# Fused forgetting attention and SwiGLU kernel: all spare TensorE matmuls left out, the order unchanged

## The chip, the cores and the metric

The kernel runs on one core of a Trainium2 chip. The metric is the device time of one execution in microseconds. The profile is of one such execution; its span is counted from the first to the last instruction.

## The reference

For each of 8 batches and 8 heads, with 576 positions of 64 values, attention with a decay that comes from a forget gate f:

```python
scores = scale * np.matmul(q, k.transpose(0, 1, 3, 2))
log_f = np.log(np.clip(f, 0.0001, 1.0))
cum = np.cumsum(log_f, axis=-1)
decay = cum[:, :, :, None] - cum[:, :, None, :]
scores = np.where(causal, -1000000000.0, scores + decay)
attn = softmax(scores)            # with 1e-09 in the denominator
attn_out = np.matmul(attn, v)
```

The heads are put side by side to x of 4608 tokens by 512, and a feed-forward layer of width 1536 follows:

```python
xn = x / np.sqrt(np.mean(x * x, axis=-1, keepdims=True) + 1e-06) * rms_g
g = xn @ w_gate
out = (g / (1.0 + np.exp(-g)) * (xn @ w_val)) @ w_out
```

Inputs and output are float32; the matmuls of the kernel run in bf16 with float32 sums.

## The kernel before, in words

The whole program is a list of 1,551 small pieces of work. Each piece (a load, a cast, a set of transposes, a block of scores, an exponential, and so on) is made by `plan.add` with its engine, an estimate of its duration, and the buffers it takes and frees. The order in which the pieces are issued is not computed when the kernel is built: it is written out in the string `ORDER` (lines 22 to 102), and `Plan.run` (line 153) goes through its words one after the other. Each engine and each DMA queue therefore works in the order of the words that belong to it; waits between engines follow from the data and the buffers.

A word has a name and may have suffixes. `@A`, `@D`, `@O` and `@S` choose the engine (ScalarE, VectorE, GpSimd, SP), `:ff` chooses a PSUM pool, and `*N` asks for spare matmuls ahead of the piece. The names that matter here, with batch first:

- `Lq`, `Lk`, `Lv`, `Lqk`: loads of q, k, v and of the last 64 positions into float32 stage tiles `st` (10 buffers), most on SP's queue, some on ScalarE's. `Lv1.3` is the load of the fourth v tile of batch 1. `Cq`, `Ck`, `Cqk`: casts of these tiles to bf16 (`ld`).
- `tr`, `trt`: transposes of q and k on TensorE (batches 0 to 2 only; lines 530, 521 and 552) into a `ff` tile; `keeptr` copies them into `QK` (line 222 by way of the helper `copy`).
- `far`: opens the PSUM tile of a block of scores of batch 0 with the causal bias, 4 matmuls (line 664). `sc`: scores of head pairs (line 679; two heads lie in the two halves of the partitions). `esc`: exponentials on ScalarE (line 688). `msc`: the causal mask on GpSimd (line 694), for batch 1 on. `sc0.0.384` holds the last block of all four head pairs in one tile, and four exponentials read it.
- `turn_dec`, `keep_dec`: the decay factors, turned on TensorE and copied to `decT` by VectorE (lines 301, 304). `Sv`: v times these factors into `Vs` (lines 451, 452), on VectorE for batch 0 and mostly on GpSimd later.
- `val`: values (line 714), `xpo`: their division into `X` by VectorE (lines 721, 722), `sq`, `rs`, `xn`: the RMS norm (lines 729, 735, 739), `xtr`: its transpose on TensorE for batches 0 and 1 (line 766), which `kxtr` copies to `xT`.
- `g`, `v…f`, `th`, `ga`, `hga`: gate and value matmuls (line 863), tanh on ScalarE, and the two products on VectorE (lines 872, 879), for groups of 512 tokens (the first two groups are halves). `pj`, `o`, `so`: the output projection (line 889), its copy and its store.
- `turn_rg`, `spread_rg`: the norm's weights turned and spread on TensorE (lines 357, 366). `wg`, `wv`, `wo`: loads of the weights by GpSimd's queue.

The first 60 us or so hold the start of the attention, where loads, casts, transposes and scores of batch 0 depend on one another. Later the feed-forward matmuls of the batches done so far fill TensorE between pieces of attention.

A piece that opens a PSUM tile calls `warm_up` (lines 249 to 253) on it. If its word has `*N`, this issues N // 4 matmuls of 512 columns and N % 4 of 128 columns on a tile `idle` of zeros. They write to the tile that the piece overwrites directly after, so they have no effect on the output. Fill for a score tile is issued where the tile is opened (`open_sc`, line 654), fill for `v0.2f` at the head of `gate` (line 858).

```python
k = st.pop("fill", 0)
for w in [4] * (k // 4) + [1] * (k % 4):
    x = bass.AP(tensor=idle.tensor, offset=idle.offset, ap=[idle.ap[0], [0, w], [1, 128]])
    nc.tensor.matmul(ps[:, 0:w * 128], lhsT=idle, rhs=x, start=True, stop=True)
```

Of the kernel before, what the change touches and what calls it, by code (L numbers as in the profile page):

```python
# [14 lines left out]
B, H, S, D = 8, 8, 576, 64  # L15
# [4 lines left out]
NP = H // 2  # L20

ORDER = """
one Lq0.0@A far Lk0.0 Lqk01 lf ident Lq0.1@A Lqk00 rg identb clear Lq0.2@A Lk0.1 far0.1.0*16 fetch_ln Ck0.0@A Lk0.2 Cq0.0 Lv0.0 tr0.01*20 clip tr0.00
log turn_rg Lv0.1 keep_rgT keeptr0.01.q keeptr0.00.k spread_rg keeptr0.01.k@D keeptr0.00.q@A Lk0.3@A scan far0.0.0 Lq0.3@A Cqk0 Cq0.1 fetch trt0*4
Lv0.40 sc0.0.0 sc0.1.0 Ck0.1 keeptrt0 Lv0.3 Cq0.2@D esc0.0.0 keep_rg@D expo Ck0.2@O far0.3.0 tr0.03 tri esc0.1.0 tr0.10 twice Lv0.41 keeptr0.03.k
turn_dec k4.0@D Lk1.0@A tr0.02 keep_dec sc4.0 Ck0.3@O keeptr0.03.q@A Lk1.1 Cq0.3@A Sv0.0 Lqk10 keeptr0.02.k@A tr0.12*8 keeptr0.10.k@D exp4.0 Lq1.0
Lv0.2@A sc0.3.0 Sv0.1@O keeptr0.12.k@D Lqk11 esc0.3.0 keeptr0.10.q sc0.0.384*4 wg0 esc0.3.384 keeptr0.02.q far0.1.1024 esc0.0.384 sc0.1.1024
esc0.1.384 wv0 esc0.2.384 val0.2.0 Lq1.1 val0.6.0:ff esc0.1.1024 far0.2.0 Lq1.3 xpo0.6.0 wg1 sc0.2.0 Lk1.3 keeptr0.12.q esc0.2.0 sc0.1.512 Sv0.4@O
val0.0.0:ff xpo0.2.0 esc0.1.512 far0.3.1024 xpo0.0.0 val0.4.0 sc0.3.1024 Sv0.3 Ck1.1@A mask4.0 far0.2.1024 Lk1.2 esc0.3.1024 sc0.2.1024 xpo0.4.0
Lv1.41 Sv0.2 sq0.1 Lq1.2 sq0.0 val0.3.2*8 Lv1.40 Cq1.0@D esc0.2.1024 val0.2.2:ff rs0.0 sc0.0.512 Ck1.0 esc0.0.512 xn0.0 far0.0.1024 sc0.0.1024 Lv1.1  # L30
Cqk1 esc0.0.1024 sc0.2.512 xn0.1 wv1 trt1*2 tr1.0 esc0.2.512 xpo0.2.2 Cq1.1 keeptrt1 xtr0.1 keeptr1.0.q@A wg2 xpo0.3.2 xtr0.0 Lq2.0 keeptr1.0.k
sc0.3.512 kxtr0.1@D val0.4.2 kxtr0.0 esc0.3.512 val0.5.2:ff k4.1@D val0.1.2:ff Cq1.3@A tr1.1 xpo0.1.2 Lv1.0 sc1.0.512 keeptr1.1.k xpo0.5.2 val0.0.2:ff
esc1.0.512 xpo0.4.2 val0.7.2:ff xpo0.0.2 val0.6.2 keeptr1.1.q@A xpo0.7.2 sc4.1 g0.0 esc1.0.0 xpo0.6.2 Ck1.3 v0.0f th0.0 sq0.3 g0.2 ga0.0 sq0.4 Ck1.2
tr1.3 exp4.1 wv2 sq0.2 keeptr1.3.q sc1.0.1024*2 th0.2 hga0.0 rs0.2 esc1.1.512 ga0.2 v0.2f*3 xn0.3 Lv1.2 keeptr1.3.k g0.4 hga0.2 Cq1.2@A xn0.2 xtr0.3
th0.4 v0.4f kxtr0.3@D esc1.0.1024 ga0.4 tr1.2 xtr0.2 keeptr1.2.q@A sc1.1.0 kxtr0.2 esc1.1.0 keeptr1.2.k@D g1.0 Sv1.4 hga0.4 esc1.1.1024 v1.0f Lv1.3
xn0.4 msc1.0.1024 th1.0 g0.6 Lk2.0@A Lqk21 ga1.0 sc1.2.512 th0.6 Lqk20 hga1.0 g1.2 esc1.2.0 ga0.6 v1.2f th1.2 esc1.2.512 ga1.2 g1.4 hga1.2 xtr0.4
Lq3.3 Sv1.1 th1.4 sc1.2.1024 kxtr0.4 Lk2.1@A ga1.4 v0.6f wo0 esc1.3.512 v1.4f hga0.6 Lq2.1 mask4.1 esc1.2.1024 g1.6 Cq2.0 hga1.4 Sv1.0 g0.8 th1.6
# [928 lines left out]
```

## Time and profile before

| what | value |
|---|---|
| median of 5 runs | 381.08 us (380.41 to 383.15) |
| the profiled execution's own time | 381.05 us |
| its span | 379.2 us |
| mean granted TensorE clock | 0.99 |
| DMA | 52.58 MB, mean 139 GB/s |
| spare matmuls (line 253) | 22, from 1.1 to 38.5 us |

The page gives busy time by engine, a row of 40 slices of the span (9.5 us each) with busy tenths and the granted clock of TensorE in tenths, and the chain of work that ended last, followed back from the last instruction. The trace can be asked for the instructions of one engine in a stretch, with the idle time ahead of each in square brackets and the instruction that ended it. Ends of matmuls are modelled: a row's length includes the way through the array, so rows of successive groups overlap. Starts are what to compare.

### The profile page before, as it was taken

How to read it: one execution, taken by the hardware profiler on the slowest of the kernel's cores; microseconds unless marked ns; L12 is line 12 of the kernel's file. 1: busy time of each engine (PE TensorE's matmuls, PEld its weight loads, DVE VectorE, ACT ScalarE, POOL GpSimd, SP SyncE). 2: the span in 40 equal slices, each digit the busy share in tenths (PEclk: the TensorE clock that was granted, in tenths of full speed). 3: DMA queues.
4: the chain of work that ended last, by engine and by line, in shares of the span. 5: the costliest groups of instructions: out<-in, count | busy, mean ns of one | idle time of the engine just before them, and what ended most of it. 6: DMA issues, size and time to landing. Idle time of an engine off the chain costs nothing.

```text
span 379.2 us, 8155 instructions
## 1 busy us (share of the span) xinstructions
PE 366.8 (97%) x3136; PEld 195.5 (52%) x3136; DVE 260.2 (69%) x500; ACT 220.2 (58%) x368; POOL 136.2 (36%) x247
## 2 busy tenths in 40 slices
PE   7889999999999999999999999999999999999996
PEld 3557778454644544455454544454445544444443
DVE  4777977849858778568856865688367876863560
ACT  4599876688696487444845585447466423323312
POOL 3763825337467144625342474021720111000001
PEclk9699999999999999999999999999999999999999
DMA  8999999996699899998959893741300234002003
GB/s 203 249 242 234 206 223 187 216 200 150 143 203 168 187 186 181 206 144 173 182 129 207 157 193 83 170 63 42 85 28 16 57 85 122 3 0 83 29 0 112
DMA packets 144774, 52.58 MB, mean 139 GB/s; under 512 B 128188, under 2 KB 141120, under 8 KB 144736
## 3 DMA queue, kind: packets, MB, share of 16 engines
q1 hardware_dynamic: 128512, 36.98, 50.3%
q0 software_dynamic: 6016, 8.79, 11.1%
q10 hardware_dynamic: 10208, 6.31, 6.8%
q8 instruction: 24, 0.39, 0.4%
q14 instruction: 14, 0.11, 0.1%
HBM read 37.90 MB, written 9.44 MB: 125 GB/s over the span
## 4 chain that ended last, share of the span: by engine, by line
PE 80%; DMA 10%; POOL 3%; DVE 2%; ACT 2%; issue 1%; SPq 0%; POOLq 0%; ACTq 0%; DVEq 0%
PE ff L863 45%; PE ff L889 22%; DMA st<-in_v_dram 5%; PE po L714 5%; PE sc L679 5%; PE ff L714 2%; DMA st<-in_k_dram 2%; DMA st<-in_q_dram 2%; DMA out_dram<-ores 1%; POOL PT L694 1%; POOL Vs L451 1%; ACT PT L688 1%; DVE xn L739 1%; PE ff L766 1%; POOL rs L735 1%
## 5 line engine op out<-in xcount | busy, mean ns | idle before, releaser
L868 ACT ACTIVATE th<-ff 128x512 f32<-128x512 f32 x108 | 64.5, 597 | 94.5 <-PE ff L863 92.0
L863 PE MATMUL ff<-xT,wv 128*128 128x512 bf16 (+1 forms) x480 | 110.9, 358 | 0.6 <-DVE ga L872 0.6
L863 PE MATMUL ff<-xT,wg 128*128 128x512 bf16 (+1 forms) x480 | 110.8, 358 | 0.4 <-ACT QK L222 0.2
L688 ACT ACTIVATE PT<-sc 128x1024 bf16<-128x1024 f32 (+2 forms) x100 | 95.7, 990 | 14.1 <-PE sc L679 13.5
L872 DVE SCALAR_TENSOR_TENSOR ga<-th,ff 128x512 f32<-128x512 f32 x108 | 73.9, 685 | 39.9 <-ACT th L868 39.1
L889 PE MATMUL ff<-wo,hT 128*128 128x512 bf16 (+1 forms) x444 | 98.2, 373 | 0.0
L879 DVE SCALAR_TENSOR_TENSOR hT<-ga,ff 128x512 bf16<-128x512 f32 x108 | 73.7, 684 | 14.8 <-PE ff L863 8.2
L863 PEld LDWEIGHTS <-wg 128*128 128x128 bf16 x480 | 45.1, 98 | 44.0 <-issue 1.9
L889 PEld LDWEIGHTS <-hT 128*128 128x128 bf16 x444 | 42.4, 98 | 47.9 <-issue 1.4
L863 PEld LDWEIGHTS <-wv 128*128 128x128 bf16 x480 | 44.5, 98 | 43.5 <-issue 3.4
L694 POOL TENSOR_SCALAR_AFFINE_SELECT PT<-PT 128x256 bf16<-128x256 bf16 (+1 forms) x84 | 42.4, 529 | 65.9 <-ACT PT L688 65.5
L714 PEld LDWEIGHTS <-PT 128*128 128x128 bf16 x896 | 33.7, 98 | 12.4 <-issue 2.1
L739 DVE SCALAR_TENSOR_TENSOR xn<-X,rs,rgb 128x512 bf16<-128x512 f32 x40 | 32.6, 842 | 7.9 <-POOL rs L735 7.8
L897 POOL DMA_DIRECT2D out_dram<-ores x16 | 9.2, 577 | 70.5 <-ACT ores L222 38.4
L222 ACT COPY ores<-ff 128x512 f32<-128x512 f32 (+1 forms) x25 | 14.2, 569 | 34.1 <-PE ff L889 30.0
L222 POOL CAST ld<-st 128x512 bf16<-128x512 f32 x32 | 21.1, 670 | 24.9 <-DMA st<-in_q_dram 14.3
L451 POOL TENSOR_TENSOR Vs<-st,decT 128x512 bf16<-128x512 f32 x21 | 23.3, 1109 | 15.1 <-DMA st<-in_v_dram 13.1
L679 PE MATMUL sc<-QK 64*128 64x256 bf16 (+3 forms) x272 | 28.5, 294 | 0.2 <-ACT PT L688 0.2
L735 POOL TENSOR_TENSOR rs<-sq,mhalf 128x5 f32<-128x5 f32 (+2 forms) x9 | 10.1, 1119 | 51.6 <-ACT junk L729 48.1
L729 ACT ACTIVATE junk<-X 128x513 bf16<-128x513 f32 x40 | 25.4, 634 | 1.7 <-DVE X L722 1.2
L714 PE MATMUL po<-Vs,PT 128*128 128x65 bf16 x577 | 24.8, 193 | 1.0 <-POOL PT L694 0.9
L679 PEld LDWEIGHTS <-QK 64*128 64x128 bf16 x528 | 13.5, 95 | 17.0 <-issue 11.9
(89 smaller groups left out, 259.1 us busy)
## 6 DMA issues: line engine op xcount, KB each, us to landing
st<-in_v_dram SPq DMA_DIRECT2D x28, 256.0 KB, 4.5
st<-in_q_dram SPq DMA_DIRECT2D x27, 256.0 KB, 4.4
st<-in_k_dram SPq DMA_DIRECT2D x26, 256.0 KB, 4.4
out_dram<-ores POOLq DMA_DIRECT2D x15, 256.0 KB, 3.4
out_dram<-ores SPq DMA_DIRECT2D x12, 256.0 KB, 2.3
out_dram<-ores ACTq DMA_DIRECT2D x8, 256.0 KB, 2.6
st<-in_k_dram ACTq DMA_DIRECT2D x6, 256.0 KB, 5.5
wo<-in_moe_w_out_dram POOLq DMA_DIRECT2D x2, 768.0 KB, 9.5
```

Source lines behind the costliest of these rows:

```text
L222: {"DVE": nc.vector.tensor_copy, "POOL": nc.gpsimd.tensor_copy, "ACT": nc.scalar.copy}[eng](o, x)
L451: e.tensor_tensor(Vs[i][:, j, :, 0:D], t, bcast(dj, D), ALU.mult)
L679: nc.tensor.matmul(sc[:, par, c:c + n], lhsT=k_cols(r, p, kj), rhs=q_cols(r, p, q0, n), start=not opened, stop=not opened or (kj, q0) == b ...
L688: nc.scalar.activation(T["pt", b, p][:, :, c0:c0 + n], T.pop(("sc", b, p, c0))[:, :, 0:n], ACT.Exp, scale=scale)
L694: nc.gpsimd.affine_select(out=d, in_=d, pattern=[[0, n], [1, 128]], compare_op=ALU.is_ge, fill=0.0, base=0, channel_multiplier=-1)
L714: nc.tensor.matmul(T["po", b, hs][:, qm, m, :], lhsT=w, rhs=Vs[i][:, kj, h, :], start=(kj == 0), stop=(kj == qi))
L739: nc.vector.scalar_tensor_tensor(xn, in0=X[i][:, j, 0:DM], scalar=T["rs", b, js][:, j:j + 1], in1=rgb, op0=ALU.mult, op1=ALU.mult)
L863: nc.tensor.matmul(ps[:, c * w:c * w + w], lhsT=wt[:, dc, (fc + c) * 128:(fc + c + 1) * 128], rhs=T["xT", g][:, dc, 0:w], start=(dc == 0), ...
L868: nc.scalar.activation(t, T["pg", g, fc], ACT.Tanh, scale=0.5)
L872: nc.vector.scalar_tensor_tensor(a, in0=T.pop(("th", g, fc)), scalar=1.0, in1=T.pop(("pg", g, fc)), op0=ALU.add, op1=ALU.mult)
L879: nc.vector.scalar_tensor_tensor(o, in0=T.pop(("ga", g, fc)).rearrange("p (c t) -> p c t", t=w), scalar=0.5, in1=T.pop(("pv", g, fc)).rear ...
L889: nc.tensor.matmul(po, lhsT=T["hT", g][:, fc, j * 128:(j + 1) * 128], rhs=wo[:, fc, c0:c1], start=(fc == 0), stop=(fc == NFC - 1))
```

## The change

All `*N` suffixes go; no word is moved, added or taken away. Nine words had one: `far0.1.0*16`, `tr0.01*20`, `trt0*4`, `tr0.12*8`, `sc0.0.384*4`, `val0.3.2*8`, `trt1*2`, `sc1.0.1024*2` and `v0.2f*3`, together 15 matmuls of 512 columns and 7 of 128. `warm_up` and the memset of `idle` stay. Cut to the words that differ:

```diff
-... far0.1.0*16 fetch_ln ... tr0.01*20 clip tr0.00
+... far0.1.0 fetch_ln ... tr0.01 clip tr0.00
-... fetch trt0*4
+... fetch trt0
-... tr0.12*8 keeptr0.10.k@D exp4.0 Lq1.0
+... tr0.12 keeptr0.10.k@D exp4.0 Lq1.0
-... sc0.0.384*4 wg0 ...
+... sc0.0.384 wg0 ...
-... val0.3.2*8 Lv1.40 ...
+... val0.3.2 Lv1.40 ...
-... trt1*2 tr1.0 ...
+... trt1 tr1.0 ...
-... sc1.0.1024*2 th0.2 ... v0.2f*3 xn0.3 ...
+... sc1.0.1024 th0.2 ... v0.2f xn0.3 ...
```

## The prediction

> **What bounds the kernel now.** I read the page first, then the chain of waits in order of time, then the stretch to 60 us engine by engine.
>
> ```profile
> PE 366.8 (97%) x3136; PEld 195.5 (52%) x3136; DVE 260.2 (69%) x500; ACT 220.2 (58%) x368; POOL 136.2 (36%) x247
> ...
> PEclk9699999999999999999999999999999999999999
> ...
> PE 80%; DMA 10%; POOL 3%; DVE 2%; ACT 2%; issue 1%; SPq 0%; POOLq 0%; ACTq 0%; DVEq 0%
> ```
>
> TensorE is busy 97% of 379.2 us, and the chain that ended last is 80% TensorE. But the spare matmuls all lie between 1.1 and 38.5 us, and there it is other things. The chain, from the view of the chain of waits (start, us, what):
>
> ```profile
> 15.13 0.50 DVE decT L304
> ...
> 16.35 0.94 DVE Vs L452
> 17.29 1.18 DVE QK L222 x2
> ...
> 36.03 19.19 DMA st<-in_v_dram
> ...
> 55.29 1.04 POOL Vs L451
> ...
> 56.49 1.29 POOL PT L694 x3
> ```
>
> From 15.13 to 18.47 it runs over VectorE without a gap, and from 36.03 to 55.22 over the load of the last v tile of batch 1 (Lv1.3). Its values are scaled and masked on GpSimd, and TensorE stands idle for them, by its timeline:
>
> ```profile
> 57.83 0.59 PE L714 MATMUL po<-Vs,PT 128*128 128x65 bf16 x14 [0.93 <-POOL PT L694]
> ```
>
> So 57.83 is pinned by a load; what TensorE gains before it is lost there, and it may fall 0.93 us behind for nothing. The load's own issue time is set by transfers: the DMA share in the table of stretches is 1.1 to 1.3 throughout 2 to 55 us. After 57.83 TensorE waits only twice for over 0.5 us, so a delay there reaches the end.
>
> TensorE's timeline around the largest fill that lies in dense work:
>
> ```profile
> 15.66 1.04 PE L253 MATMUL ff<-idle 128*128 128x512 bf16 x2
> 16.49 0.83 PE L540 MATMUL ff<-ident,ld 128*128 128x128 bf16 x8
> 17.25 0.34 PE L679 MATMUL sc<-QK 64*128 64x256 bf16 x4
> 17.52 0.39 PE L253 MATMUL sc<-idle 128*128 128x512 bf16 x1
> 17.92 0.29 PE L679 MATMUL sc<-QT,QK 64*128 64x64 bf16 x8
> 18.52 0.29 PE L679 MATMUL sc<-QT,QK 64*128 64x64 bf16 x8 [0.30 <-DVE QK L222]
> ```
>
> Even with two fills ahead of it, the second half of sc0.0.384 still waits for VectorE, till 18.47.
>
> The clock, in stretches (us, TensorE busy, granted clock, DMA share, GB/s):
>
> ```profile
> 3.28:6.70 3.42, 3.31 (x16) 1.00 1.19 267
> 6.70:10.11 3.41, 1.58 (x12) 1.00 1.23 268
> 10.11:13.52 3.41, 2.59 (x22) 0.50 1.27 258
> 13.52:16.94 3.42, 3.42 (x28) 0.50 1.26 242
> 16.94:20.35 3.41, 3.03 (x54) 1.00 1.21 251
> ```
>
> The clock falls to half at 10.11 and returns at 16.94 (from shares 0.61 and 0.56 in the half-microseconds that hold the edges). The 1.00 of the first row is not to be believed: a 512-column spare matmul takes 0.61 us (median 615 ns in the ff tiles) there and 384 ns at 23.7, and eight transposes take 1.00 us at 5.87 and 0.61 at 28.13. The far blocks take 0.85 us at 2.77 and 0.49 at 8.50: half clock to about 6.7, full from there to 10.11, half to 16.94, full to the end.
>
> **What the Trainium skill says.** "TensorE: Matmul & The Clock Gate", Part 1: the default is half rate; a busy window of 3413 ns raises the clock, an idle one lowers it, and the windows run freely, so the edge shifts against the kernel's start from run to run. The trace agrees: the two edges lie 6.83 us apart, two windows of 3.41. The window before 16.94 was 100% busy and was followed by full rate, the one before that (76%) was not, and the 46% one was followed by half rate. Part 4 of that page says that transposes don't engage the gate as matmuls do. The trace does not bear this out: in the stretch that ended with the rise at 16.94, most of the work is transposes (L540, L301). Same page, "Back-to-back issue gap": 512 columns cost 427 ns cold and 216 warm; the trace has 0.83 us for two at 15.66 (half clock), 0.44 for two at 23.70.
>
> **The change part by part.** In the built instruction lists, 22 matmuls and their 22 weight loads vanish from TensorE (15 of 512 columns, 7 of 128). The other engines' lists are the same; waits that fills carried pass to the next real instruction. Nothing is added, and no DMA or queue is moved. By fill, from start of the fill to the next start:
>
> 1. far0.1.0 (4, 1.09 to 2.77): far could start when ident is ready (weights at 2.46), 0.3 us earlier. Its tile is next needed at 10.89. Worth 0.
> 2. tr0.01 (5, 3.41 to 5.75): the transposes then wait for GpSimd's cast, done at 5.81. Worth 0.
> 3. trt0 (1, 8.83 to 9.21): then idle to 10.35 for a cast. Worth 0. But without fills 1 and 2 no window before 10.11 is full, so 6.70 to 10.11 runs at half clock. Three things lie there: rgT, spread_rg (0.65 us) and far0.0.0 (0.49). At half clock they end at most 1.14 us later, 10.1 instead of 8.99: still before 10.35, also without the 0.38 of the fill. Cost 0; cover left 0.2 us.
> 4. tr0.12 (2, 0.83 us) and sc0.0.384 (1, 0.40): the transposes could start at 15.66, since their casts ended by 14.90. sc0.3.0 then ends near 16.9 and its exponential on ScalarE (17.63 now) comes 0.7 earlier. But both halves of sc0.0.384 need VectorE's two QK copies, 17.29 to 18.47, which follow decT at 15.13 without a gap. So ScalarE's next exponential still starts at 18.85, and ScalarE has no gap from there to 34. Worth 0.
> 5. val0.3.2 (2, 0.44): followed at 26.40 by a wait of 0.86 for ScalarE. Worth 0.
> 6. trt1 (2 small, 0.25): then a wait of 0.18 for X (VectorE, 28.87). sc1.0.1024 (2 small, 0.21): then a wait of 0.72 for hT. Worth 0.
> 7. v0.2f (3 small, 38.29 to 38.47): TensorE does come 0.18 us earlier, if wv1 has landed (issued at 27.79, 9.2 us for its size: 37.0). It loses that at 57.83, where 0.93 becomes 1.11. Worth 0; at best 0.18.
>
> Sum of the occupied time of 4 to 7: 0.83 + 0.40 + 0.44 + 0.25 + 0.21 + 0.18 = 2.31 us, of which nothing reaches the end.
>
> **The clock's price.** TensorE is dense now from 12.29 to 18.2 (5.9 us); without fills 4 from 12.29 to about 16.9 (4.6 us), then 1.0 us of idle for VectorE. A stretch of L us holds a whole 3.41 us window, wherever the windows fall, with chance (L - 3.41)/3.41: 0.73 now, 0.35 then, more if a nearly full window counts. With this trace's phase, 13.52 to 16.94 would just stay full. Otherwise the rise comes a window later, about 20.4. Then far0.1.1024, sc0.1.1024 and two values at half clock end some 0.85 us later (half clock adds 0.50 + 0.35 + 0.36 + 0.35 = 1.56 at most, and ScalarE's seven exponentials from 18.85 to 22.64 cover about half), and so does ScalarE's row after them. The 0.93 at 57.83 covers that. So the unknown is 0 at the low end; at the high end two windows: 6.82 us at half rate do 3.41 of the some 5.6 us of work there (3.03 + 3.03 less fills), a lag of 2.2 us. I take 0.2 for the likely case, what a lag of 0.85 to 1.1 leaves beyond 0.93.
>
> The profiled run took 381.05 us (span 379.2 and 1.85 around it), the median of the five is 381.08, so no correction. Likeliest: 381.05 + 0 + 0.2 = 381.3.
>
> **The rivals.**
> Slower: the clock rises late. Without the 1.23 us of fill 4, no full window lies before the dense work from 18.5 on, and ScalarE's unbroken row from 18.85 to 34 passes on what TensorE loses. For it: 76% was not enough in this trace, and the 383.15 among the five runs (2 us over the others) would fit a missed window. Against it: 0.93 us of cover. It decides once two windows are missed and the loads don't absorb it: 381.05 + 2.2 = 383.3.
> Faster: the fills stand in front of real work on the engine that is 97% busy. All 2.31 us of 4 to 7 come off: 378.7. Against it: each is followed by a wait for another engine.
> Third: loads re-time. Casts that come earlier or later free stage buffers, and Lv1.3 lands elsewhere than 55.22. With DMA saturated, I put it at 1 us either way: 380 to 382.1.
> That the change doesn't do what it says is excluded by the instruction lists.
>
> **How the numbers follow.** Under 0.5% (1.9 us, about what a measurement of this kernel can tell from no change) lie all times from 379.2 to 383.0. Likeliest case 0.62, within. Re-timed loads 0.10, 0.01 of it outside on each side. Late clock 0.24, slower. Fills on the path 0.04, faster. Hence faster 0.05, same 0.70, slower 0.25. The range leaves out the fast rival and takes in the slow one and a little of a third missed window: 380.2 to 383.6.
>
> **What would show it.** Right: ScalarE's first exponential of sc0.0.384 again at about 18.85; the wait at 57.83 grown or shrunk but 57.83 itself within 0.5 us; DVE's QK copies at 17.3; half clock up to at least 16.9 without the full-rate stretch at 6.7 to 10. Slow rival: half clock beyond 20.4 and the first values of batch 1 after 58.5. Fast rival: TensorE's work at 57.83 starting 1 us or more earlier. I am wrong if the load that ends at 55.22 moves by over 1 us, or if the clock falls again later than 24 us.

## The result, and the profile after

| | before | after |
|---|---|---|
| median | 380.82 us (378.90 to 384.69, 79 runs) | 381.96 us (380.96 to 385.80, 44 runs) |
| ratio to before | | 1.0029, 95% interval 1.0017 to 1.0040 |
| profiled execution, its span | 381.05, 379.2 us | 382.96, 381.1 us |

Leaving the spare matmuls out makes the kernel 0.29% slower, some 1.1 us: within the 0.5% of the forecast case, though not by the forecast 0.2 us. The profiled execution lies 1.0 us above its median, so the two traces show the mechanism larger than the medians do. The same rows of the page after:

```profile
PE 364.1 (96%) x3114; PEld 195.0 (51%) x3114; DVE 262.2 (69%) x500; ACT 220.4 (58%) x368; POOL 136.5 (36%) x247
...
PEclk9999999999999999999999999999999999999999
...
PE 83%; DMA 8%; DVE 3%; ACT 2%; issue 1%; SPq 1%; POOL 1%; ACTq 0%; DVEq 0%; POOLq 0%
```

TensorE is busy 2.7 us less and the end is later. The clock row says 9 throughout, where before it had a 6. That is not good news: as in the first 6.7 us of the kernel before, half clock that no recorded change precedes is shown as full. Only durations tell. TensorE's timeline after (start, length in us, line, tiles, count; in square brackets the idle time ahead and what ended it):

```profile
15.84 0.42 PE L630 MATMUL sc<-QT,K 128*128 128x64 bf16 x4
16.80 1.03 PE L540 MATMUL ff<-ident,ld 128*128 128x128 bf16 x8 [0.54 <-ACT ld L222]
17.77 0.50 PE L679 MATMUL sc<-QK 64*128 64x256 bf16 x4
18.34 0.39 PE L679 MATMUL sc<-QT,QK 64*128 64x64 bf16 x8
18.94 0.40 PE L679 MATMUL sc<-QT,QK 64*128 64x64 bf16 x8 [0.20 <-DVE QK L222]
19.27 0.82 PE L664 MATMUL sc<-far,ident 128*128 128x256 bf16 x4
...
21.21 0.83 PE L664 MATMUL sc<-far,ident 128*128 128x256 bf16 x4
...
23.38 0.80 PE L664 MATMUL sc<-far,ident 128*128 128x256 bf16 x4
...
24.73 0.50 PE L664 MATMUL sc<-far,ident 128*128 128x256 bf16 x4
```

The far blocks, the same four matmuls each time, take 0.82, 0.83 and 0.80 us and only the last one 0.50: half clock to nearly 24 us, where the kernel before had full clock from 16.94. Two further things are seen here. The transposes of tr0.12 wait 0.54 us for ScalarE's cast of a late q load, where a fill stood before. And sc0.0.384 still waits for VectorE, at 18.94 as it did at 18.52; the 0.42 between them is older (the first q load landed at 9.44 instead of 8.88). So what the late clock costs comes after this point, by ScalarE's timeline, first before, then after:

```profile
18.85 3.79 ACT L688 ACTIVATE PT<-sc 128x256 bf16<-128x256 f32 x7 [0.41 <-PE sc L679]
```

```profile
19.38 2.32 ACT L688 ACTIVATE PT<-sc 128x256 bf16<-128x256 f32 x5 [0.26 <-PE sc L679]
22.52 1.72 ACT L688 ACTIVATE PT<-sc 128x768 bf16<-128x768 f32 x2 [0.82 <-PE sc L679]
```

The row of seven exponentials that had no gap before now has one of 0.82 us, for scores that TensorE made at half clock. By xtr0.1, the first transpose of the normed x, the stage is 1.78 us behind, 1.36 of it not explained by the load; before and after:

```profile
28.92 0.71 PE L766 MATMUL ff<-ident,xn 128*128 128x128 bf16 x8 [0.18 <-DVE X L722]
```

```profile
30.70 0.71 PE L766 MATMUL ff<-ident,xn 128*128 128x128 bf16 x8 [0.18 <-DVE X L722]
```

And then the lag is not covered. GpSimd's row for the last two v tiles of batch 1, and TensorE at their first values, both after:

```profile
49.46 1.04 POOL L451 TENSOR_TENSOR Vs<-st,decT 128x512 bf16<-128x512 f32 x1 [1.61 <-DMA st<-in_v_dram]
50.59 1.04 POOL L451 TENSOR_TENSOR Vs<-st,decT 128x512 bf16<-128x512 f32 x1
```

```profile
58.52 0.58 PE L714 MATMUL po<-Vs,PT 128*128 128x65 bf16 x14
...
61.10 1.03 PE L863 MATMUL ff<-xT,wv 128*128 128x256 bf16 x8 [0.36 <-DVE ga L872]
```

Lv1.3 is scaled at 50.59 without a wait (55.29 before, after 5.84 us of waiting), and the values at 58.52 wait for nothing. The 0.93 us of idle that was to absorb the lag is no longer there. The first projection starts 1.25 us later than before (68.55 to 67.30), and from there to the end of the span it is 312.55 and 311.9 us: the other 0.65 us of the 1.9 between the two spans arises later, and isn't explained.

### The profile page after: what moved, and what is told of

Same layout as the page of the kernel before. It is cut to its first block, busy times and chain, and to the rows that moved or that the text cites. A ratio compares the mean times of both kernels' runs of the same rounds, so it can differ in the third digit from the quotient of the medians.

```text
span 381.1 us, 8113 instructions
## 1 busy us (share of the span) xinstructions
PE 364.1 (96%) x3114; PEld 195.0 (51%) x3114; DVE 262.2 (69%) x500; ACT 220.4 (58%) x368; POOL 136.5 (36%) x247
## 3 DMA queue, kind: packets, MB, share of 16 engines
HBM read 37.90 MB, written 9.44 MB: 124 GB/s over the span
## 4 chain that ended last, share of the span: by engine, by line
PE 83%; DMA 8%; DVE 3%; ACT 2%; issue 1%; SPq 1%; POOL 1%; ACTq 0%; DVEq 0%; POOLq 0%
PE ff L863 47%; PE ff L889 22%; PE sc L679 5%; PE po L714 4%; DMA st<-in_k_dram 3%; PE ff L714 2%; DMA st<-in_q_dram 2%; DMA st<-in_v_dram 2%; DMA QK<-ld 1%; DVE ga L872 1%; PE ff L528 1%; DVE xn L739 1%; PE ff L766 1%; ACT th L868 1%; DVE hT L879 1%
## 5 line engine op out<-in xcount | busy, mean ns | idle before, releaser
L735 POOL TENSOR_TENSOR rs<-sq,mhalf 128x5 f32<-128x5 f32 (+2 forms) x9 | 10.1, 1119 | 51.3 <-ACT junk L729 46.4
L451 POOL TENSOR_TENSOR Vs<-st,decT 128x512 bf16<-128x512 f32 x21 | 23.3, 1109 | 11.2 <-DMA st<-in_v_dram 9.5
```

## The experiments

My theory before the runs: only the clock after 17 us matters, the fills of tr0.12 and sc0.0.384 set it, and all other fills are worth nothing. The rivals: the fills of the first 10 us count; the fills act as pacing, not by the clock; the fills stood in the way. Each edit is against the kernel after unless another is named; no kernel leaves out or changes any part of the reference's computation. Each had five rounds beside the kernel before; ratios are to that.

**1. Only the middle fills.**

```diff
-tr0.12
+tr0.12*8
-sc0.0.384
+sc0.0.384*4
```

> Only the fills ahead of tr0.12 and in sc0.0.384 are put back (3 spare matmuls of 512 columns, 1.2 us). Theory (the clock rises late without them, and that is all that costs): the dense stretch on TensorE is whole again, the clock rises near 17 to 18 us as in the kernel before, and the time is that of the kernel before, 0.3% below the changed kernel (ratio to before 1.000, within 0.15%). Rival (the early fills count too, because they warm the stretch from 6.7 to 10.1 us): the time stays near the changed kernel's, ratio 1.002 to 1.004.

Measured: 381.32 us, ratio 1.0024 (1.0010 to 1.0038). The theory missed. The profiled execution is a good one (381.0 us): the clock rises at about 17.4, its first gate matmul is at 33.83 (33.69 before). But the median is not: the middle fills make a timely rise possible. That they don't make it certain would fit the median and isn't shown: in executions of this kernel the first rise is on no record. The ratio is the rival's, that the early fills count too.

**2. Only the fills of the first 10 us.**

```diff
-far0.1.0
+far0.1.0*16
-tr0.01
+tr0.01*20
-trt0
+trt0*4
```

> Only the fills of the first 10 us are put back (far0.1.0, tr0.01, trt0: 10 spare matmuls). Theory: they give full clock from about 6.7 to 10.1 us, which is covered by loads and casts, and the clock still rises late the second time: ratio to before 1.003, as the changed kernel. Rival (the early warm stretch matters): ratio 1.000.

Measured: 381.71 us, ratio 1.0028 (1.0013 to 1.0044), as the theory had it. Here the first rise comes before 6 us, so the clock's later fall and rise are on record (stretch, TensorE busy, granted clock, DMA share, GB/s):

```profile
8.00:9.00 1.00, 0.99 (x7) 0.67 1.23 287
9.00:10.00 1.00, 0.91 (x5) 0.50 1.25 279
10.00:17.00 7.00, 5.76 (x49) 0.50 1.26 254
17.00:20.00 3.00, 2.50 (x34) 0.50 1.23 257
20.00:21.00 1.00, 1.00 (x18) 0.50 1.27 194
21.00:22.00 1.00, 1.00 (x10) 0.51 1.28 238
```

Half clock from about 8.3 to 22.0 us, four windows of 3.41 us, though TensorE was busy 83% of 10 to 20 us (5.76 and 2.50 of 10).

**3. Only the late fills.** `val0.3.2*8`, `trt1*2`, `sc1.0.1024*2` and `v0.2f*3` put back.

> Only the fills from 23 us on are put back (val0.3.2, trt1, sc1.0.1024, v0.2f: 2 of 512 and 7 of 128 columns, 0.9 us of TensorE's time). Theory: worth nothing either way, ratio to before 1.003 as the changed kernel; the two before val0.3.2 could speed up a late rise a little, by up to 0.2 us. Rival (they stand in front of real work, so the changed kernel gains from leaving them out): ratio 1.004 to 1.006.

Measured: 381.69 us, ratio 1.0035 (1.0018 to 1.0051). Worth nothing measurable by themselves. The median lies 0.27 us below that of the kernel after, so nothing shows them standing in the way, though the interval reaches into the rival's range.

**4. More fills early, to hold the clock.** Against the kernel before:

```diff
-turn_rg
+turn_rg*12
-far0.0.0
+far0.0.0*12
-trt0*4
+trt0*16
-tr0.03
+tr0.03*4
```

> All fills of the kernel before, and more in the gaps from 6.9 to 10.3 us (3 of 512 columns each at turn_rg and far0.0.0, 4 instead of 1 at trt0, 1 at tr0.03), so that the window from 6.7 to 10.1 us is nearly full. Theory of the clock: it does not fall at 10.1; the transposes and decay factors from 12.3 to 15.1 us, which stand ahead of VectorE's unbroken row, run at full clock and end some 1 us earlier, so ratio to before 0.997 to 0.999, with the clock full from 7 us on. Rival (loads and casts set this stretch, the clock is only a symptom): same time as before, ratio 1.000, although the clock stays full.

Measured: 379.95 us, ratio 0.9996 (0.9975 to 1.0018), which by itself does not tell the two apart. The trace does. The clock stays full, and the stretch that I had taken as given shrinks; TensorE's timeline:

```profile
12.77 0.83 PE L540 MATMUL ff<-ident,ld 128*128 128x128 bf16 x12
13.53 0.52 PE L301 MATMUL po<-ident_f,PT 64*128 64x64 f32 x5
...
16.87 0.29 PE L679 MATMUL sc<-QT,QK 64*128 64x64 bf16 x8 [0.31 <-DVE QK L222]
```

The twelve transposes take 0.83 us instead of 1.48, and sc0.0.384 gets its copies at 16.87 instead of 18.52. VectorE's row was pinned in part by TensorE's half clock ahead of it: the copy of the decay factors (decT) starts at 14.33 instead of 15.13. The other half of the 1.65 us is not the clock's. It is VectorE's cast into Vs (L452), which takes 0.18 us here and 1.02 before. GpSimd and VectorE before:

```profile
15.71 1.54 POOL L451 TENSOR_TENSOR Vs<-st,decT 128x512 bf16<-128x512 f32 x1 [1.74 <-DVE decT L304]
```

```profile
16.26 1.02 DVE L452 CAST Vs<-decT 128x8 bf16<-128x8 f32 x1
```

In the 11 traces in which GpSimd starts to scale its v tile (L451) 0.2 us or more ahead of this cast, the cast takes 1.02 or 1.03 us and ends 0.03 to 0.05 us after GpSimd's instruction (before at 17.28 and 17.25). In 4 GpSimd waits for its v tile until 15.81, the cast is done at 15.64; in 7 the two start 0.14 us apart, cast first. All 13 traces agree in this, but no run was made to test it.

**5. The same time, without columns.** The kernel before, with its fills made of one-column matmuls:

```diff
-        for w in [4] * (k // 4) + [1] * (k % 4):
-            x = bass.AP(tensor=idle.tensor, offset=idle.offset, ap=[idle.ap[0], [0, w], [1, 128]])
-            nc.tensor.matmul(ps[:, 0:w * 128], lhsT=idle, rhs=x, start=True, stop=True)
+        for _ in range(k * 5 // 3):
+            nc.tensor.matmul(ps[:, 0:1], lhsT=idle, rhs=idle[:, 0:1], start=True, stop=True)
```

> The kernel before, with each spare matmul of 512 columns replaced by six or seven of one column (one for each of the small ones): about the same time on TensorE at half clock, but next to no columns streamed. Clock theory: if the gate looks at streamed columns, the early rise at 6.7 us is gone and the second rise is late, ratio to before 1.002 to 1.004, as the changed kernel. Rival (pacing: the fills help because they hold the pieces behind them back): ratio 1.000, wherever the clock rises. If weight loads and instructions count as activity, the clock rises as before and the run doesn't tell the two apart.

Measured: 381.30 us, ratio 1.0031 (1.0015 to 1.0048): as without fills. In its trace (line numbers are one lower there) the far blocks are still at half clock at 23.55:

```profile
16.25 0.51 PE L252 MATMUL ff<-idle 128*128 128x1 bf16 x13
16.63 1.01 PE L539 MATMUL ff<-ident,ld 128*128 128x128 bf16 x8
...
23.55 0.80 PE L663 MATMUL sc<-far,ident 128*128 128x256 bf16 x4
...
25.10 0.50 PE L663 MATMUL sc<-far,ident 128*128 128x256 bf16 x4
```

The thirteen hold tr0.12 back by 0.38 us where the two large ones took 0.83, so pacing was copied by half; what they do not do is raise the clock. The early ones also fill less time, 0.85 and 1.07 us where the large ones take 1.89 and 2.34, so the first rise may be missing because TensorE is less busy. The later stretch is nearly full: from 12.89 to 24.9 TensorE is busy for 11.58 of 12.01 us by the trace, and the window of 3.41 us to 18.13, counted back from the rise near 24.95, has no idle time at all. Still no rise follows it. This speaks against pacing, and with the traces it leaves the clock.

**6. Early and middle fills, no late ones.** The kernel before without the four late fills.

> The kernel before without the fills from 23 us on (val0.3.2, trt1, sc1.0.1024, v0.2f). Each part alone left the time 0.24 to 0.35% above before. Theory (the parts of the first 18 us act together: the early rise and the dense stretch to 17 us each save half-clock windows, and the late fills are worth nothing): ratio to before 1.000, within 0.15%. Rival (the late fills matter after all): ratio 1.002.

Measured: 380.96 us, ratio 1.0004 (0.9980 to 1.0027). The interval holds both expectations; the point is nearer the theory's. With 1 it suggests that the early fills do count beside the middle ones: without them 1.0024, with them 1.0004 (the intervals overlap). Its profiled execution, the fastest of its 14, shows how they can: the clock is full until 12.6 and half only to 16.0, one window instead of two.

**7 and 8. The held clock, without late fills, and without middle ones as well.** Experiment 4 without the late fills, and then also without those of experiment 1.

> The heavier fills of the first 11 us and those ahead of tr0.12 and in sc0.0.384, without the fills from 23 us on. Theory: clock full from about 7 us on, the time 0.0 to 0.3% below before (ratio 0.997 to 1.000), first gate matmuls near 32.1 us instead of 33.7, and part of that lost again by 67 us. Rival (late fills are needed): ratio 1.002.

Measured: 379.99 us, ratio 0.9986 (0.9970 to 1.0001), within the expectation. The first gate matmul is at 32.73, not near 32.1: the clock is full, but tr0.12 waits 1.34 us for a cast, whose load is late.

> Only the heavier fills of the first 11 us (and one at tr0.03), none ahead of tr0.12, in sc0.0.384 or later. Theory (a clock once full is kept by the work itself, which fills half to three quarters of each window): same as with them, ratio 0.997 to 1.000. Rival (the clock falls again at some 13 us and comes back late): ratio 1.002 to 1.004, with half clock visible in the trace after 10 us.

Measured: 380.30 us, ratio 0.9997 (0.9980 to 1.0014): the mean lies with the theory, but its trace shows the rival's fall, later than expected. In the gap that the middle fills had, TensorE waits for a cast, and by 17.16 it is at half clock:

```profile
16.35 0.62 PE L540 MATMUL ff<-ident,ld 128*128 128x128 bf16 x8 [1.67 <-ACT ld L222]
16.90 0.34 PE L679 MATMUL sc<-QK 64*128 64x256 bf16 x4
17.16 0.39 PE L679 MATMUL sc<-QT,QK 64*128 64x64 bf16 x8
...
18.14 0.80 PE L664 MATMUL sc<-far,ident 128*128 128x256 bf16 x4
```

**9. More at tr0.12.** As 7, with `turn_rg*16` and `tr0.12*20`.

> The heavier early fills (4 matmuls of 512 columns at turn_rg, 3 at far0.0.0, 4 at trt0, 1 at tr0.03) and 5 instead of 2 ahead of tr0.12, where the kernel with the clock held waited 1.3 us for a cast; none from 23 us on. Theory: fewer executions let the clock fall, so the time is below the kernel before by 0.1 to 0.4% (ratio 0.996 to 0.999), with first gate matmuls at 32 to 33 us. Rival (in executions in which the clock does fall, the added 1.3 us at half clock delay the transposes): ratio 1.000 to 1.002.

Measured: 379.86 us, ratio 0.9977 (0.9964 to 0.9990). In its trace the clock falls once more, from 25.8 to 29.2 us, and the first gate matmul is at 33.28, later than the expected 32 to 33.

**10. No fills before 6 us.**

```diff
-turn_rg
+turn_rg*8
-far0.0.0
+far0.0.0*8
-trt0
+trt0*8
-tr0.12
+tr0.12*8
-sc0.0.384
+sc0.0.384*4
```

> No fills before 6 us; 2 matmuls of 512 columns each at turn_rg, far0.0.0 and trt0, and those ahead of tr0.12 (2) and in sc0.0.384 (1); none later. The clock can't rise at 6.7 us then, at the earliest near 10 us. Theory (what counts is full clock from about 12 to 24 us, not the stretch from 6.7 to 10.1): ratio to before 0.999 to 1.001. Rival (the fills of the first 6 us are needed for it, as with the kernel that had only the middle ones): ratio 1.002 to 1.003.

Measured: 380.55 us, ratio 1.0000 (0.9985 to 1.0015). With six spare matmuls from 6.6 to 11.3 us the time is that of the kernel with ten at 1 to 9 us: the far block at 9.99 takes 0.85 us, the twelve transposes at 13.17 take 0.83, so the rise lies between.

**11. The clock held to 28 us.** As 9, with `val0.3.2*8` and `trt1*4`.

> The fills of the kernel with ratio 0.9977 (more early ones, 5 ahead of tr0.12), and those ahead of val0.3.2 (2 of 512 columns) and trt1 (1 of 512) as well, because that kernel's profiled execution lost the clock once more from 25.8 to 29.2 us, after a stretch of 0.3 and 0.9 us gaps. Theory (each half-clock window costs some 0.5 us at the end): ratio to before 0.996 to 0.998, with no half clock after 17 us and the first gate matmul 0.5 us earlier in its trace. Rival (after 24 us ScalarE and VectorE bind, and half clock there is free): ratio 0.998, no better than without them.

Measured: 379.62 us (378.74 to 380.60), ratio 0.9969 (0.9955 to 0.9983), better than both kernels of the study. The gate matmuls start at 32.92 instead of 33.28 as in 9, and no half clock is seen after 17 us. The interval holds the rival's 0.998 too, so a gain over 9 isn't shown.

**The traces side by side** (us; starts read from TensorE's timelines; the second column is the time by which full clock is reached for good, from recorded changes or from the durations):

| profiled execution | full clock by | first gate matmul | first values of batch 1 (wait ahead) | first projection | span |
|---|---|---|---|---|---|
| 11, held to 28 | 7 | 32.92 | 55.97 | 66.08 | 378.1 |
| 4, more early | 7 | 32.05 | 55.00 | 65.70 | 378.1 |
| 7, more early, no late | 7 | 32.73 | 55.60 | 65.62 | 377.9 |
| 10, none before 6 us | 12 | 33.32 | 57.55 (1.01) | 67.03 | 378.4 |
| 6, early and middle | 16.0 | 32.61 | 55.67 | 65.69 | 377.0 |
| before | 16.9 | 33.69 | 57.83 (0.93) | 67.30 | 379.2 |
| 1, middle | 17.4 | 33.83 | 56.90 | 66.92 | 379.1 |
| 8, more early alone | 20.6 (full till 17.1) | 33.90 | 56.95 | 66.98 | 378.0 |
| 2, early | 22.0 | 34.87 | 57.92 | 67.96 | 379.7 |
| 3, late | 22 | 34.86 | 57.91 | 67.95 | 380.1 |
| after | 24 | 35.47 | 58.52 | 68.55 | 381.1 |
| 5, one column | 25 | 35.86 | 58.91 | 68.94 | 380.3 |
| 9, as 7, more at tr0.12 | 29.2 (full till 25.8) | 33.28 | 56.33 | 66.35 | 377.8 |

In the main, the later full clock comes, the later the first gate matmul. Where it comes by 17 us the order is not kept: loads move the start as well. ScalarE's cast for tr0.12 starts at 13.62 in 6 and at 14.45 in 4, but at 15.48 in 7 and 15.59 in 11, where it waits for its load for over 1.5 us. From the gate matmul the values follow after 22.9 to 23.1 us wherever no load holds them. Some 24.2 us it is in the two with a wait. From the first projection to the end it is 311.0 to 312.6 us in all of them.

**Executions of one kernel sorted by clock.** Each execution has its mean recorded clock; 1 minus it, times twice the span of 379 us, over 3.41 us, is the number of half-clock windows after the first rise. The kernel before, in all its executions beside the experiments: one window 379.9 us (median of 47), two 380.6 (95), three 380.6 (46). Experiment 2: one window 379.3 (3 executions), two 381.2 (7), three 381.6 (5), four 382.1 (5), five 382.3 (2). Experiment 11: none in 21 of 22, 379.5. The instructions are the same within each of these rows. But nothing was set here: loads also land at other times in each execution, and may move the clock and the time together, so this goes with the table and doesn't prove it. Between one window and two lies a clear step in the kernel before, between two and three none. With so few executions the steps of experiment 2 are rough, but their direction is that of the table.

## Why the prediction was right or wrong

Right in its case (within 0.5%), and in the mechanism that decides: the direct value of the fills is nil, and their price is the clock. The sizes are not confirmed by that: 0.2 us was forecast and 1.1 measured, and with or without its cover the sum stays under 0.5%. The base hid part of the miss: 381.05 was taken, and 79 executions have 380.82, so 381.3 lies only 0.7 under 381.96. By its steps:

1. Fills 1 to 3 (before 10 us) worth nothing: right for what stands directly behind them, and alone they gain nothing (2). Beside fill 4 they seem worth some 0.2%: 1 lies 0.24% over the kernel before, which differs by them and by the late fills, and 6 without the late ones lies at 0.04%. This the prediction put at 0. Others at 6.6 to 11.3 us do as well (10). And the stretch from 10.1 to 15 us at half clock was taken as given, because the trace of before had it. It costs: with it at full clock, the decay factors reach VectorE 0.8 us earlier (4), and the clock held from 7 to 28 us is worth 0.31% (11). The prediction's steps never priced this.
2. Fill 4: the wait for VectorE behind it was right for the change: it is there before and after. In 1, 7, 9 and 11, where TensorE comes later, it is all but gone. Wrong was "the transposes could start at 15.66, since their casts ended by 14.90": after the change the cast waits for its load and TensorE waits 0.54 us for the cast. The fill had covered a wait that this one trace did not have. And the fill alone does not bring the time back (1).
3. Fills 5 to 7 worth 0: nothing in 3 and 6 speaks against it, as far as their intervals go. In a kernel that holds the clock, those at val0.3.2 and trt1 do serve; 9 and 11 differ by 0.08% with overlapping intervals, so that is seen in the trace and not shown in the time.
4. The clock's price: the lag was right and its cover wrong. The likely case took 0.2 us, "what a lag of 0.85 to 1.1 leaves beyond 0.93". Measured is 1.1 us at the median; in the traces the lag is 1.36 us (after) and 1.18 us (2: 30.10 against 28.92 at xtr0.1, with the same 18.52 ahead of it). Nothing of the 0.93 was left. "So 57.83 is pinned by a load" was the failing step: the load is not a fixed point. In 11 of the 12 traces other than that of before, the first values of batch 1 follow the gate matmuls without waiting for the load of Lv1.3 (in 1 it lands late too, with the masks behind it just in time); only in 10 do they wait again. What decides whether Lv1.3 lands at some 50 or at 55 us was not tried and stays open. When its issue ends doesn't decide it alone: at 46.32 before, at 41.56 after, but at 45.39 in 6, which doesn't wait either. I had put the re-timing of loads at 1 us either way; it was almost 5, and it worked by removing a wait, not by adding one. Over 1 us was the prediction's own sign of being wrong, and 57.83 moved by 0.69 where it allowed 0.5: by its own signs this step fails, though the case holds.
5. The slow rival is the one that came about in the profiled execution: half clock beyond 20.4, values at 58.52. Its full price of 2.2 us for two windows, reckoned as if TensorE had no idle time to catch up in, is too high: 1.36 us by 30.7.
6. The fast rival (2.31 us on the path) fell: removing the late fills alone gains nothing (6), and the change as a whole loses.

That transposes don't count for the clock gate, which the Trainium skill has in "TensorE: Matmul & The Clock Gate", Part 4, was doubted in the prediction from one window. The runs leave that open, but do not contradict it as the prediction thought. In 2 and 3 the clock did not rise by 17 us, with a gap of 0.31 and 0.35 us before tr0.12. In 5 one-column matmuls fill that gap, and the full window to 18.13, mostly transposes, was not followed by a rise either. In 1, with the large fills in that place, it was, as in the kernel before. No run has a window of transposes only, and where the windows of 5 fall is counted back over two of them.

## What to carry to other kernels

Spare matmuls in front of a wait cost nothing measurable here and can be worth the clock; their worth is not where they stand but what runs at half clock afterwards, so price the clock of every stretch on the path, also of one that is at half clock in the kernel as it is. Idle time ahead of an instruction is no cover unless what ends it stands still when everything before it moves. And where the clock's windows fall differs by execution: one trace shows one case, so sort the executions by their recorded clock before saying what a change of some tenths of a per cent did.

## What the runs showed of the hardware

- A TensorE that is busy 83% of the time (10 to 20 us in experiment 2, by the durations that the trace models) can stay at half clock for four windows.
- The clock falls without any long gap: in experiment 8 with gaps of at most 1.67 us, in 9 (at 25.8 us) with gaps of at most 0.87 us.
- One-column matmuls, 59 of them within the first 4.2 us, at some 30 ns each, do not raise the clock (5); nine of 512 columns do (before). The nine also keep TensorE busy for 4.2 us and the 59 for 1.9, so it is open whether columns or time make the difference.
- A window that the trace shows fully busy is not always followed by full clock: 3.41 of 3.41 us to 18.13 in experiment 5, with transposes, scores and one-column matmuls, and the rise came near 24.95.
- VectorE's cast at L452 takes 0.18 us, or 1.02 to 1.03 where GpSimd's instruction at L451 is under way, and then ends 0.03 to 0.05 us after it (11 of 13 traces).
- Half clock before the first rise is on no record: the clock row and the mean clock of such an execution say 1.00. Only durations show it.
